# First slice of a two-layer block: chunk 5's masks and scaling moved ahead of lot 3's sign, and lower weights ahead of the next lot's sign

## The chip, the cores and the metric

The kernel runs on one core of a Trainium2 chip. The metric is the device time of one execution in microseconds (us). Before the change it is 591.01 us, the median of three runs (590.67 to 591.92).

Engines are named as the profile names them: PE is TensorE (matmuls; PEld its weight loads), DVE is VectorE, ACT is ScalarE, POOL is GpSimd, and SP issues most DMAs.

## What is computed

A linear attention with decay runs over 4 sequences of 8 heads and 768 positions. Its output, 3072 tokens by 512, goes through two matrix products with a squared ReLU between them.

```
for b in range(nb):                       # blocks of positions, per head
    intra = (qb @ kb.T * Dmask) @ vb      # Dmask[i, j] = lam ** (i - j) for i >= j
    inter = (qb * lam_pow) @ kv_state
    out[b] = intra + inter
    kv_state = lam_block * kv_state + (kb * rev_pow).T @ vb
x = out reshaped to (3072, 512)
g = relu(x @ w_in) ** 2                   # 3072 x 2048
return g @ w_out                          # 3072 x 512
```

## The kernel before

Positions are handled in chunks of 128, 6 to a sequence and 24 in all, and tokens in slices of 4 chunks (512 tokens). Each slice runs 16 iterations f over blocks of the 2048 hidden features: `hidden` (12 matmuls, line 521) makes h, `square` (ACT, lines 528 to 531) makes gh and the exact square, `rest` (DVE, line 536) their difference gl, and `project` (lines 551, 552, 556), one iteration later, adds to four output tiles. Every operand is held as a high and a low part (wh and wl, xh and xl, gh and gl), and three products are taken of them. A chunk's attention is spread over the iterations of the slice ahead: `scores` after step 0, `masked` (two masks on DVE, line 302, from PSUM) in step 1, `attend` in step 2.

The first slice (this loop, about 26 to 125 us) also splits the weights as they arrive, in 17 lots u, with u = f + 2 in iteration f. For a lot, SP loads `raw` (line 113); ACT takes the absolute value of its high words into A (`first_hi`, line 118) and scales the low words (`first_lo`, line 123); DVE works on A in four steps, `clamp` (L131), `shift` (L135), `sign` (L142) and `rounded` (L148), each of which needs the one before it; ACT then writes wh (`upper`, L154), and DVE wl = A - wh (`lower`, L157). `raw` and A have two buffers each, so lot u + 2 is loaded when rounded is done with lot u.

Each engine runs its instructions in the order in which this file issues them; nothing reorders them. The order is written out by hand. For f < 3 an iteration issues lower of the lot before, then clamp, shift, sign and rounded of its own lot, and upper after `rest`; from f = 3 on it issues clamp, shift and sign, then upper and lower of the lot before, then rounded.

POOL scales k and q of a chunk in place (`prep_k`, L296, and `prep_q`, L290) and the state (`decay`, L376). Where it may begin is held back by `turn` (L162), a copy of one element into `mark` on POOL: for f = 1 of A of the iteration's own lot, from f = 3 on of the lower weights just made. It stands ahead of the scaling in POOL's queue, so the scaling waits for what turn waits for. Chunk 4's scaling belongs to f = 1, chunk 5's q scaling to f = 5, chunk 6's k scaling to f = 8, and chunk 7's to f = 12 (k) and f = 13 (q).

Of the kernel before, what the change touches and what calls it, by code (L numbers as in the profile page):

```python
# [31 lines left out]
NLOT = NF + 1  # L32
# [3 lines left out]
def body(ctx: ExitStack, tc: tile.TileContext, qT, kT, kvq, lam, w, out):  # L36
# [31 lines left out]
    def load_qk(t):  # L68
        if t in (2, 3):
            lent[t] = wk.tile([P, 2, KT * C, 2], F32, name=f"lent{t}", tag=("xh", "xl")[t - 2])  # L70
            x = lent[t][:, 0].rearrange("p a b -> p (a b)")
        elif (t, 0) in lent:
            x = lent[t, 0]
        else:
            x = io.tile([P, 2 * DM], F32, name="qk_sb")
        feat[t] = x.rearrange("p (k a b) -> p k a b", k=2, a=NPR)
        for k, y in enumerate((kT, qT)):
            nc.sync.dma_start(out=feat[t][:, k], in_=y[t])

    def load_kv(t):  # L80
        if t in (2, 3):
            x = lent[t][:, 1].rearrange("p a b -> p (a b)")
        elif (t, 1) in lent:
            x = lent[t, 1]
        else:
            x = io.tile([P, 2 * DM], F32, name="kv_sb")
        nc.sync.dma_start(out=x, in_=kvq[t, :, 0 : 2 * DM])
        x = x.rearrange("p (k h d) -> p k h d", k=2, h=H)
        tok[t] = x[:, 0], x[:, 1]
# [8 lines left out]
    def lot(t, u):  # L98
        if u in (0, NF):
            return t[:, u : u + 1]  # L100
        return t.rearrange("p (s f) d -> p s f d", s=2)[:, :, u]
# [6 lines left out]
    def wload(u):  # L108
        if u < NLOT:
            x = pieces(u)  # L110
            raw[u] = wk.tile([P, len(x) * DM], I64, name="raw", tag="raw")
            for i, (side, f) in enumerate(x):
                nc.sync.dma_start(out=raw[u][:, i * DM : (i + 1) * DM], in_=w[side, :, f])

    def first_hi(u):
        r = raw.pop(u).bitcast(U32).rearrange("p (n two) -> p n two", two=2)
        A = wk.tile([P, r.shape[1]], U32, name="A")
        nc.scalar.activation(A.bitcast(F32), r[:, :, 1].bitcast(F32), AF.Abs)
        cv[u] = r[:, :, 0], r[:, :, 1], A

    def first_lo(u):
        L = cv[u][0]
        nc.scalar.activation(L, L, AF.Copy, scale=2.0**-29)
# [5 lines left out]
    def clamp(u):  # L129
        A = cv[u][2].bitcast(F32)  # L130
        V.tensor_scalar(out=A, in0=A, scalar1=2.0**-15, scalar2=float(LIM), op0=ALU.max, op1=ALU.min)  # L131

    def shift(u):
        A = cv[u][2]
        V.tensor_scalar(  # L135
            out=A, in0=A, scalar1=3, scalar2=0x3FFFFFFF,
            op0=ALU.logical_shift_left, op1=ALU.bitwise_and,
        )

    def sign(u):  # L140
        L, Hw, A = cv[u]
        V.scalar_tensor_tensor(  # L142
            out=A, in0=Hw, scalar=0xC0000000, in1=A, op0=ALU.bitwise_and, op1=ALU.bitwise_or
        )

    def rounded(u):
        L, Hw, A = cv[u]
        V.tensor_tensor(out=A, in0=A, in1=L, op=ALU.add)  # L148

    def whole(u):  # L150
        return cv[u][2].bitcast(F32).rearrange("p (a d) -> p a d", d=DM)

    def upper(u):
        nc.scalar.copy(lot(wh, u), whole(u))  # L154

    def lower(u):
        V.tensor_tensor(out=lot(wl, u), in0=whole(u), in1=lot(wh, u).bitcast(F32), op=ALU.subtract)  # L157
        cv.pop(u)

    def turn(u, half):  # L160
        x = cv[u][2].bitcast(F32)[0:1, 0:1] if half else wl[0:1, u, 0:1].bitcast(F32)
        nc.gpsimd.tensor_copy(mark[:, 0:1], x)  # L162
# [43 lines left out]
    for j in range(2):  # L206
# [5 lines left out]
        lambda o, x, y, op=op: V.tensor_tensor(out=o, in0=x, in1=y, op=op)  # L212
# [5 lines left out]
    b_, t_, u_, c_, d_, af = (sq[:, i, 0 : NS - 1] for i in range(6))  # L218
# [69 lines left out]
    def prep_q(t):  # L288
        if t % NCB:
            nc.gpsimd.tensor_tensor(out=feat[t][:, 1], in0=feat[t][:, 1], in1=qpow, op=ALU.mult)  # L290

    def prep_k(t):
        if t % NCB < NCB - 1:
            x = tok[t][0].rearrange("p (a j) d -> p a j d", j=2)
            y = mask.rearrange("p j a c -> p a j c")[:, :, :, C - 1 : C]
            nc.gpsimd.tensor_tensor(out=x, in0=x, in1=y.broadcast_to([P, NPR, 2, D]), op=ALU.mult)  # L296

    def masked(t):
        a_of[t] = []
        for j in range(2):  # L300
            a = wk.tile([P, NPR, C], F32, name="a", tag="gl" if t in (1, 3) else "a")
            V.tensor_tensor(
                out=a, in0=sc_of[t][j].rearrange("p (a b) -> p a b", a=NPR),
                in1=mask[:, j], op=ALU.mult,
            )
            a_of[t].append(a)
# [57 lines left out]
    def attend(t, pool, name):  # L364
        u = pool.tile([P, DM], F32, name=name)
        o = pool.tile([P, DM], F32, name=name)
        news(t, u)
        within(t, o, True, not t % NCB)
        before(t, o, False, True)
        update(t, u)  # L370
        return split(t, o)

    def decay(t):
        if t % NCB < NCB - 2:
            for j, r in enumerate(rows):
                nc.gpsimd.tensor_tensor(  # L376
                    out=kvd[r], in0=kv[r, :, rows[j]],
                    in1=qpow[r, :, C - 1 : C].broadcast_to([D, NPR, D]), op=ALU.mult,
                )
# [128 lines left out]
    def fade_state(second):  # L508
        d = kv[:, :, D:] if second else kv[:, :, 0:D]
        nc.gpsimd.tensor_tensor(  # L510
            out=kvd, in0=d, in1=qpow[:, :, D - 1 : D].broadcast_to([P, NPR, D]), op=ALU.mult
        )
# [3 lines left out]
    def hidden(m, f, xh, xl):  # L516
        h = ps_h.tile([P, N], F32, name="h")
        k = 0
        for wt, x in ((wh, xh), (wl, xh), (wh, xl)):
            for kt in range(KT):  # L520
                nc.tensor.matmul(  # L521
                    h, wt[:, f, kt * P : (kt + 1) * P], x[:, kt], start=k == 0, stop=k == 11
                )
                k += 1
        return h

    def square(h):
        nc.scalar.activation(h, h, AF.Relu)  # L528
        gh = wk.tile([P, N], F32R, name="gh")
        nc.scalar.activation(gh, h, AF.Square)  # L530
        nc.scalar.activation(h, h, AF.Square)  # L531
        return gh

    def rest(m, f, r, gh):
        gl = wk.tile([P, N], F32R, name="gl")
        V.tensor_tensor(out=gl, in0=r, in1=gh.bitcast(F32), op=ALU.subtract)  # L536
        g_of[m, f] = gh, gl
# [528 lines left out]
    for f in range(NF):  # L1066
        t, step, u_ = G + f // 4, f % 4, f + 2
        h = hidden(0, f, *xs_of[0])
        if f < 3:
            lower(u_ - 1)  # L1070
            for op in (clamp, shift, sign, rounded):
                op(u_)
            if f == 1:
                turn(u_, True)
        else:
            if u_ < NLOT:
                for op in (clamp, shift, sign):
                    op(u_)
            if f > 3:
                upper(u_ - 1)  # L1080
            lower(u_ - 1)
            if u_ - 1 < NF:
                turn(u_ - 1, False)
            if u_ < NLOT:
                rounded(u_)
        wload(u_ + 2)
        if f == 3:
            low[G]()
        if f == 0:
            decay(3)  # L1090
        if step == 0 and f or f == 1:
            prep_k(t)
        if step == 1:
            prep_q(t)
        if step == 3:
            if t < 2 * G - 1:
                decay(t)
            else:
                fade_state(False)
        gh = square(h)  # L1100
        rest(0, f, h, gh)
        if step == 1:
            masked(t)
        if f < 3:
            upper(u_)
            first_hi(u_ + 1)
        if step == 2:
            low[t] = attend(t, ps_a, "att")
            if t > G:
                low[t]()  # L1110
        if u_ + 1 < NLOT:
            if f >= 3:
                first_hi(u_ + 1)
            first_lo(u_ + 1)
        if prev is not None:
            project(*prev)
        prev = (0, f)
        if step == 2:
            load_qk(t + 2)
            load_kv(t + 2)  # L1120
        if step == 0:
            scores(t, ps_a, "att")
        if f == NF - 2:
            fold_mask()
            scale_k(t + 1)
        if f == NF - 1:
            open_half(t + 1)
            scale_k(t + 2)
# [30 lines left out]
    for f in range(NF):  # L1159
        t = first_t + f // 2  # L1160
# [54 lines left out]
    for f in range(NF):  # L1215
        t = first_t + f // 2
# [96 lines left out]
```

## Time and profile before

| | |
|---|---|
| median of 3 runs | 591.01 us |
| the profiled execution | 592.3 us |
| its span, first to last instruction | 590.5 us |
| granted TensorE clock over the span | 0.995 |
| DVE busy, 48.54 to 78.43 us | 29.52 of 29.89 us |
| DVE busy, 79.96 to 121.00 us | 40.52 of 41.04 us |

A row of a timeline gives the start in us from the span's start, the duration, the engine, the line of the kernel, the operation, output and inputs with their shapes, and how many instructions the row joins. A bracket at its end gives the time for which the engine sat idle ahead of it, and who released it. In a row of stretches each number is an engine's busy time, in the order PE, PEld, DVE, ACT, POOL; the clock, DMA's busy share and GB/s follow.

### The profile page before, as it was taken

What the parts mean: (1) busy time and instruction counts of PE and PEld (TensorE: products, weight loads), DVE (VectorE), ACT (ScalarE), POOL (GpSimd) and SP (SyncE); (2) the same over time, 40 slices, a digit from 0 to 9 for tenths busy, and PEclk for the clock granted to TensorE, in tenths of its full rate; (3) what the DMA queues carried; (4) which work ended last, traced back from release to release, by engine and by line L of the source; (5) the groups of instructions that cost most, each with busy time, mean ns of one, the idle gap of its engine ahead of it and who ended that gap; (6) DMA issues with size and microseconds to landing.
All of it is one profiled execution on the core that took longest, in us unless ns stands there. A gap on an engine that the chain in (4) does not pass through costs nothing.

```text
span 590.5 us, 12541 instructions
## 1 busy us (share of the span) xinstructions
PE 573.2 (97%) x5006; PEld 484.6 (82%) x5006; DVE 416.0 (70%) x684; ACT 272.3 (46%) x501; POOL 97.5 (17%) x106
## 2 busy tenths in 40 slices
PE   8989999999899999999999999999899999999996
PEld 6877887888788887878888887888688888999996
DVE  6899989956567675786666667577554456997943
ACT  4676876835254455433333334445533233642520
POOL 4420221433323231000000002355100000000000
PEclk9999999999899999999999999999999999999999
DMA  8766475326778695466666644632287665766863
GB/s 294 301 225 215 157 258 196 138 74 243 247 233 286 198 299 211 146 203 204 197 195 197 196 161 148 229 128 73 73 279 240 196 194 175 255 214 209 280 206 108
DMA packets 69386, 119.32 MB, mean 202 GB/s; under 512 B 6352, under 2 KB 30928, under 8 KB 69328
## 3 DMA queue, kind: packets, MB, share of 16 engines
q1 hardware_dynamic: 67152, 116.42, 60.1%
q10 hardware_dynamic: 2176, 2.10, 1.0%
q8 instruction: 40, 0.66, 0.4%
q14 instruction: 18, 0.15, 0.1%
HBM read 88.08 MB, written 29.36 MB: 199 GB/s over the span
## 4 chain that ended last, share of the span: by engine, by line
PE 75%; DVE 12%; issue 6%; ACT 3%; DMA 2%; POOL 1%; DVEq 0%; SPq 0%; POOLq 0%; ACTq 0%
PE h L681 17%; PE h L521 10%; PE acc L920 7%; PE acc L551 7%; PE acc L556 7%; PE acc L552 7%; PE att L681 7%; PE att L920 4%; PE att L442 3%; PE h L920 2%; DVE A L142 2%; DVE sums L212 1%; DVE A L148 1%; DVE wl L157 1%; DVE rec L212 1%
## 5 line engine op out<-in xcount | busy, mean ns | idle before, releaser
L551 PE MATMUL acc<-wh,gh 128*128 128x512 f32 x256 | 101.1, 395 | 0.0
L556 PE MATMUL acc<-wh,gl 128*128 128x512 f32 x256 | 99.9, 390 | 0.0
L552 PE MATMUL acc<-wl,gh 128*128 128x512 f32 x256 | 99.7, 390 | 0.0
L681 PE MATMUL h<-wh,ring 128*128 128x512 f32 x320 | 85.9, 390 | 0.6 <-DVE kv_sb L212 0.5
L528 ACT ACTIVATE h<-h 128x512 f32<-128x512 f32 x48 | 28.0, 583 | 99.6 <-PE h L521 40.2
L681 PEld LDWEIGHTS h<-wh,ring 128*128 128x128 f32 x320 | 59.8, 188 | 14.1 <-DVE kv_sb L212 1.3
L536 DVE TENSOR_TENSOR gl<-h,gh 128x512 fp32r<-128x512 f32 x48 | 32.9, 686 | 36.5 <-ACT h L531 36.5
L551 PEld LDWEIGHTS acc<-wh,gh 128*128 128x128 f32 x256 | 48.0, 188 | 10.9 <-issue 0.5
L556 PEld LDWEIGHTS acc<-wh,gl 128*128 128x128 f32 x256 | 48.1, 188 | 10.8 <-DVE gl L536 0.6
L552 PEld LDWEIGHTS acc<-wl,gh 128*128 128x128 f32 x256 | 48.1, 188 | 9.6
L681 PE MATMUL h<-wl,ring 128*128 128x512 f32 x160 | 49.3, 389 | 0.0
L510 POOL TENSOR_TENSOR kvd<-kv,qpow 128x256 f32<-128x256 f32 x27 | 23.2, 861 | 88.1 <-DVE kv L212 73.2
L521 PE MATMUL h<-xh,wh 128*128 128x512 f32 x128 | 36.5, 408 | 0.3 <-DVE a L212 0.2
L393 POOL TENSOR_TENSOR kv_sb<-kv_sb,mask 128x512 f32<-128x512 f32 x13 | 16.0, 1231 | 124.3 <-DMA kv_sb<-in_kvq 124.1
L521 PE MATMUL h<-xh,wl 128*128 128x512 f32 x128 | 34.6, 392 | 0.7 <-DVE wl L157 0.7
L920 PE MATMUL acc<-folds,wh 128*128 128x256 f32 x192 | 35.2, 283 | 0.0
L681 PEld LDWEIGHTS h<-wl,ring 128*128 128x128 f32 x160 | 30.0, 188 | 6.3
L521 PE MATMUL h<-xl,wh 128*128 128x512 f32 x128 | 34.2, 389 | 0.0
L681 PE MATMUL att<-wh,ring 128*128 128x512 f32 x128 | 34.2, 389 | 0.0
L212 DVE TENSOR_TENSOR wl<-sums,wh 128x1024 fp32r<-128x1024 f32 x24 | 29.2, 1218 | 2.4 <-ACT wh L892 1.9
L920 PEld LDWEIGHTS acc<-folds,wh 128*128 128x128 f32 x192 | 30.0, 192 | 0.0
L530 ACT ACTIVATE gh<-h 128x512 fp32r<-128x512 f32 x48 | 28.8, 600 | 1.5
(251 smaller groups left out, 1188.0 us busy)
## 6 DMA issues: line engine op xcount, KB each, us to landing
ring<-ws SPq DMA_DIRECT2D x112, 256.0 KB, 3.0
raw<-in_w SPq DMA_DIRECT2D x32, 512.0 KB, 4.4
folds<-wt SPq DMA_DIRECT2D x64, 256.0 KB, 3.6
kv_sb<-in_kvq SPq DMA_DIRECT2D x19, 512.0 KB, 6.0
ws<-parts SPq DMA_DIRECT2D x32, 256.0 KB, 3.8
qk_sb<-in_kT SPq DMA_DIRECT2D x20, 256.0 KB, 4.0
qk_sb<-in_qT SPq DMA_DIRECT2D x20, 256.0 KB, 4.4
out_x<-o SPq DMA_DIRECT2D x16, 256.0 KB, 5.1
```

The lines of the kernel that those rows point to most:

```text
L212: lambda o, x, y, op=op: V.tensor_tensor(out=o, in0=x, in1=y, op=op)
L442: nc.tensor.matmul(o[h][r, p * D : (p + 1) * D], x, y, start=(h, r.start) not in begun, stop=end, skip_group_check=True,)
L510: nc.gpsimd.tensor_tensor(out=kvd, in0=d, in1=qpow[:, :, D - 1 : D].broadcast_to([P, NPR, D]), op=ALU.mult)
L521: nc.tensor.matmul(h, wt[:, f, kt * P : (kt + 1) * P], x[:, kt], start=k == 0, stop=k == 11)
L528: nc.scalar.activation(h, h, AF.Relu)
L530: nc.scalar.activation(gh, h, AF.Square)
L536: V.tensor_tensor(out=gl, in0=r, in1=gh.bitcast(F32), op=ALU.subtract)
L551: nc.tensor.matmul(accs[m][i], gh[:, cs], wh[:, j], start=f == 0, stop=False)
L552: nc.tensor.matmul(accs[m][i], gh[:, cs], wl[:, j], start=False, stop=False)
L556: nc.tensor.matmul(accs[m][i], gl[:, cs], wh[:, j], start=False, stop=end)
L681: nc.tensor.matmul(bank, x[:, part_, kt], t[:, q + kt], start=start and z == 0, stop=stop and z == 5, skip_group_check=True,)
L920: nc.tensor.matmul(bank[:, r * 2 * P : (r + 1) * 2 * P], x, y, start=n == 0 and r == 0 and z == 0, stop=n == NQ - 1 and z == 2, skip_group ...
```

## The change

In f = 1 chunk 4's masks (called the fifth chunk in the change's own words, counted from one) and the turn that lets POOL scale its k and q stand right behind lot 3's shift, ahead of its sign and rounded; they were behind rounded and, for the masks, behind gl. From f = 3 on lower of the lot before stands ahead of the own lot's sign instead of behind it. No instruction is added or removed.

```diff
         if f < 3:
             lower(u_ - 1)
-            for op in (clamp, shift, sign, rounded):
-                op(u_)
+            clamp(u_)
+            shift(u_)
             if f == 1:
                 turn(u_, True)
+                masked(t)
+            sign(u_)
+            rounded(u_)
         else:
             if u_ < NLOT:
-                for op in (clamp, shift, sign):
-                    op(u_)
+                clamp(u_)
+                shift(u_)
             if f > 3:
                 upper(u_ - 1)
             lower(u_ - 1)
+            if u_ < NLOT:
+                sign(u_)
             if u_ - 1 < NF:
                 turn(u_ - 1, False)
             if u_ < NLOT:
                 rounded(u_)
...
         rest(0, f, h, gh)
-        if step == 1:
+        if step == 1 and f > 1:
             masked(t)
```

On DVE, in f = 1, lot 3's steps with the masks (`a`) of chunk 4; rows with - are those of before, with + those of the change:

```order
 L131 TENSOR_SCALAR A<-A 128x1024
 L135 TENSOR_SCALAR A<-A 128x1024
-L142 SCALAR_TENSOR_TENSOR A<-raw,A 128x1024
-L148 ISA A<-raw,A 128x2048
-L536 TENSOR_TENSOR gl<-h,gh 128x512
 L302 TENSOR_TENSOR a<-att,mask 128x512 x2
+L142 SCALAR_TENSOR_TENSOR A<-raw,A 128x1024
+L148 ISA A<-raw,A 128x2048
+L536 TENSOR_TENSOR gl<-h,gh 128x512
 L157 TENSOR_TENSOR wl<-A,wh 128x2x512
```

The two masks go past sign, rounded and gl; ahead of lower (L157), which needs ACT's upper of the same lot, there is now gl alone.

On DVE, in f = 5, before the change; A of the first two rows is lot 7's, and `wl` is made from lot 6:

```order
L131 TENSOR_SCALAR A<-A 128x1024
L135 TENSOR_SCALAR A<-A 128x1024
L142 SCALAR_TENSOR_TENSOR A<-raw,A 128x1024
L157 TENSOR_TENSOR wl<-A,wh 128x2x512
L148 ISA A<-raw,A 128x2048
L536 TENSOR_TENSOR gl<-h,gh 128x512
L302 TENSOR_TENSOR a<-att,mask 128x512 x2
```

The same place with the change:

```order
L131 TENSOR_SCALAR A<-A 128x1024
L135 TENSOR_SCALAR A<-A 128x1024
L157 TENSOR_TENSOR wl<-A,wh 128x2x512
L142 SCALAR_TENSOR_TENSOR A<-raw,A 128x1024
L148 ISA A<-raw,A 128x2048
L536 TENSOR_TENSOR gl<-h,gh 128x512
L302 TENSOR_TENSOR a<-att,mask 128x512 x2
```

Lower and sign have changed places, so rounded now stands right behind the sign that it needs. The turn is released by lower, as before. The order on PE, ACT, POOL and SP is the same as before; what changes there is when the instructions they wait for are done.

## The prediction

> **What bounds the kernel now.** I read the page's busy shares first, then busy time by stretches, then each engine's timeline from 29 to 121 us, where the changed loop runs.
>
> ```profile
> PE 573.2 (97%) x5006; PEld 484.6 (82%) x5006; DVE 416.0 (70%) x684; ACT 272.3 (46%) x501; POOL 97.5 (17%) x106
> ...
> 29.00:52.00 23.00, 21.33 (x140) 17.06 (x138) 21.04 (x24) 16.97 (x23) 3.48 (x5) 1.00 0.63 219
> 52.00:121.00 69.00, 68.33 (x413) 55.14 (x414) 66.64 (x80) 52.64 (x69) 17.99 (x18) 1.00 0.54 185
> ...
> 40.17 0.69 PE L317 MATMUL att<-kv_sb 128*64 128x64 f32 x16 [1.67 <-POOL kv_sb L296]
> 52.41 1.19 PE L521 MATMUL h<-xh,wl 128*128 128x512 f32 x4 [0.41 <-DVE wl L157]
> 54.86 0.19 PEld L556 LDWEIGHTS acc<-wh,gl 128*128 128x128 f32 x1 [0.32 <-DVE gl L536]
> 66.83 1.12 PE L325 MATMUL att<-a,kv_sb 128*64 128x128 f32 x15
> ```
>
> Over the whole span PE is the bound. In this loop that average misleads: a stretch lists busy PE, PEld, DVE, ACT and POOL, and DVE works 21.04 of 23.00 us and 66.64 of 69.00. PE waits 1.67 us for the scaled k (at 40.17), 0.41 for lower weights and 0.32 for gl, all of them released by DVE or by POOL after its turn, which DVE releases. The row at 66.83 has no wait, but the masks that it reads (65.64 in a fence below) end at 65.64 + 1.28 = 66.92, just as it starts. PE has no slack there: what DVE is late at chunk 5's masks, PE is late. Taking away PE's 1.67 us is a gain only if DVE also reaches the later points earlier.
>
> **Step 1, f = 1: masks, turn and scaling ahead of lot 3's sign.**
>
> ```profile
> 35.55 0.69 DVE L135 TENSOR_SCALAR A<-A 128x1024 uint32<-128x1024 uint32 x1
> 36.28 1.23 DVE L142 SCALAR_TENSOR_TENSOR A<-raw,A 128x1024 uint32<-128x1024 uint32 x1
> 37.64 1.23 DVE L148 CUSTOM_DVE_ANT_0 A<-raw,A 128x2048 uint16<-128x2048 uint16 x1
> 38.78 0.68 DVE L536 TENSOR_TENSOR gl<-h,gh 128x512 fp32r<-128x512 f32 x1
> 39.38 1.28 DVE L302 TENSOR_TENSOR a<-att,mask 128x512 f32<-128x512 f32 x2
> 40.58 1.87 DVE L157 TENSOR_TENSOR wl<-A,wh 128x1024 fp32r<-128x1024 f32 x1
> 42.37 0.68 DVE L131 TENSOR_SCALAR A<-A 128x1024 f32<-128x1024 f32 x1
> ...
> 38.93 0.17 POOL L162 COPY mark<-A 1x1 f32<-1x1 f32 x1 [8.80 <-DVE A L148]
> 39.07 1.05 POOL L296 TENSOR_TENSOR kv_sb<-kv_sb,mask 128x512 f32<-128x512 f32 x1
> 40.08 1.28 POOL L290 TENSOR_TENSOR qk_sb<-qk_sb,qpow 128x512 f32<-128x512 f32 x1
> ...
> 38.90 1.05 ACT L154 CAST wh<-A 128x1024 fp32r<-128x1024 f32 x1 [1.56 <-DVE A L148]
> ...
> 21.80 1.05 POOL L296 TENSOR_TENSOR lent<-lent,mask 128x512 f32<-128x512 f32 x1
> 21.82 2.13 DVE L142 SCALAR_TENSOR_TENSOR A<-raw,A 128x1024 uint32<-128x1024 uint32 x1
> ...
> 144.17 1.96 DVE L212 TENSOR_TENSOR parts<-sums,parts 128x1024 fp32r<-128x1024 f32 x1
> 145.00 1.60 POOL L510 TENSOR_TENSOR kvd<-kv,qpow 128x256 f32<-128x256 f32 x1
> 146.05 1.64 DVE L212 TENSOR_TENSOR rec<-wh,wl 128x1024 f32<-128x1024 f32 x1
> ```
>
> Nothing is removed; the question is what lies beside what. The last five rows show that DVE and POOL block each other. A sign that starts while POOL scales takes 2.13 us, not 1.23, and ends 23.95 - 22.85 = 1.10 after POOL. From 144 us they take turns: POOL's row at 145.00 ends (146.60) 0.47 after the DVE instruction that it waited behind (146.13), and the next one on DVE, started at 146.05, ends 1.09 after POOL. So what POOL has queued gets in at the end of a DVE instruction, ahead of the next. The masks read PSUM and are not stretched (1.28 beside the scaling at 39.07). Before, the k scaling and the first half of the q scaling lie beside gl and masks, and the rest of the q scaling stretches one lower to 1.87 (0.65 lost).
>
> After: the masks start 0.60 after the shift, as at 38.78 to 39.38, so at 36.15; the sign follows 1.20 later at 37.35. Its new wait for the turn costs nothing: the turn (0.17 us) runs beside the masks, and so does the k scaling. But the q scaling (1.28 us) is now due at about 37.45, and DVE has only sign and rounded to do, both on SBUF. Uncontended, rounded starts 1.36 after the sign, as 36.28 to 37.64. The loss by the q scaling lies between 0 (POOL always gives way) and 1.28 (all of it); I take 1.0, nearest to the 0.90 that the shorter scaling cost at 21.82. Rounded then ends at 37.35 + 1.36 + 1.0 + 1.23 = 40.94. ACT's upper (1.05) was hidden behind gl and masks; now only gl covers it. With 0.03 us for each handover, as 38.87 to 38.90, lower starts at 42.05; an unstretched lower occupies DVE for 1.14 (62.77 to 63.91 below), so the next clamp starts at 43.19 instead of 42.37: **+0.8** (bounds -0.2 to +1.1). PE gets its scaled k early, but then waits for gl and lower weights, which are later. Behind the later rounded, SP also issues the raw load of lot 5 later:
>
> ```profile
> 38.89 0.80 SPq L113 DMA_DIRECT2D raw<-in_w  x2
> raw<-in_w SPq DMA_DIRECT2D x32, 512.0 KB, 4.4
> 47.39 1.11 ACT L118 ACTIVATE A<-raw 128x1024 f32<-128x1024 f32 x1
> ```
>
> About 2.1 us later it lands near 38.89 + 2.1 + 4.4 = 45.4, still ahead of its reader at 47.39: nothing.
>
> **Step 2, f = 3 to 13: lower ahead of sign.** The pattern before, at f = 5, with POOL and ACT beside it:
>
> ```profile
> 60.90 0.69 DVE L135 TENSOR_SCALAR A<-A 128x1024 uint32<-128x1024 uint32 x1
> 62.77 1.22 DVE L157 TENSOR_TENSOR wl<-A,wh 128x1024 fp32r<-128x1024 f32 x1
> 63.91 1.22 DVE L148 CUSTOM_DVE_ANT_0 A<-raw,A 128x2048 uint16<-128x2048 uint16 x1
> 65.64 1.28 DVE L302 TENSOR_TENSOR a<-att,mask 128x512 f32<-128x512 f32 x2
> ...
> 64.12 1.04 POOL L162 COPY mark<-wl 1x1 f32<-1x1 f32 x1 [4.42 <-DVE wl L157]
> 65.12 1.30 POOL L290 TENSOR_TENSOR qk_sb<-qk_sb,qpow 128x512 f32<-128x512 f32 x1
> ...
> 60.78 1.03 ACT L154 CAST wh<-A 128x1024 fp32r<-128x1024 f32 x1
> ```
>
> Shift start to rounded start is 63.91 - 60.90 = 3.01 us. After: lower follows the shift, on which it does not depend, in 0.60, then sign in 1.14, then rounded, which needs that sign, in 1.36: 3.10. That is 0.09 a lot, 11 lots: **+1.0** (bounds 0 to 1.3). PE gets lower weights some 1.2 us earlier, which ends its 0.41 us wait; but gl and masks, which come after rounded, are later, so this counts nothing.
>
> Lower needs ACT's upper, and the sign no longer covers it. At f = 5 upper ends at 61.81 and lower would start at 60.90 + 0.60 = 61.50: 0.3 us lost, 0.25 after DVE's added 0.09. At f = 8:
>
> ```profile
> 79.96 0.69 DVE L131 TENSOR_SCALAR A<-A 128x1024 f32<-128x1024 f32 x1 [1.52 <-ACT A L118]
> 80.69 0.70 DVE L135 TENSOR_SCALAR A<-A 128x1024 uint32<-128x1024 uint32 x1
> 80.86 1.05 ACT L154 CAST wh<-A 128x1024 fp32r<-128x1024 f32 x1
> 84.91 1.05 POOL L296 TENSOR_TENSOR kv_sb<-kv_sb,mask 128x512 f32<-128x512 f32 x1
> 85.43 1.09 DVE L131 TENSOR_SCALAR A<-A 128x1024 f32<-128x1024 f32 x1
> ```
>
> Upper ends at 81.91, lower would start at 81.29: 0.65. Together **+0.9** (bounds 0 to 1.0). DVE's 1.52 us of idle time at 79.96 absorbs nothing: it waits for a raw load that is issued behind an earlier rounded, which is later as well.
>
> **Step 3: POOL's turn comes 1.2 us earlier in the lot.** At 64.12 the turn, released by lower, is held by rounded (1.04 us instead of 0.17), so the q scaling starts at 65.12, when DVE goes over to gl and masks from PSUM. After, the instruction behind lower is the sign. The turn is held until the sign ends; then DVE pauses 0.13 us (1.36 - 1.23) before rounded, and POOL's scaling gets in first, as POOL did at 146.1 with no pause at all. Rounded waits for it: 1.28 less what the pause and the start hide, about 1.0 at f = 5 and at f = 13: **+2.0** (bounds 0 to 2.6). The k scaling at f = 8 and f = 12 (1.05) costs about 0.8 in the same way, where before it stretched a clamp by 0.40 (1.09 for 0.69): **+0.8** (bounds -0.8 to 1.3).
>
> No row has rounded itself starting under POOL; the nearest is the sign. A rule speaks to it: the Trainium skill, "SBUF — State Buffer", "Who interferes with whom", says that a DVE instruction with two SBUF inputs contends with a GpSimd instruction that reads SBUF, and that whichever issues first holds the pair for its whole length. By it, rounded (two SBUF inputs) is blocked in full and the sum below stands or rises by the 0.3 that I took off each q scaling; if rounded were exempt, the sum would be near 1.5. The trace agrees where it can: 2.13 us for a sign, 1.28 for masks.
>
> The last masks that bind are those of chunk 7:
>
> ```profile
> 116.52 1.28 DVE L302 TENSOR_TENSOR a<-att,mask 128x512 f32<-128x512 f32 x2
> 118.04 1.04 PE L325 MATMUL att<-a,kv_sb 128*64 128x128 f32 x16
> ```
>
> They end at 117.80, so PE has 0.24 of slack: -0.2. **Sum**: 0.8 + 1.0 + 0.9 + 2.0 + 0.8 - 0.2 = +5.3 us, which PE carries on, as it is 97% busy. The profiled execution took 592.3 us (span 590.5), 1.3 above the median of 591.0; against it the sum is 597.6, against the median **596.3 us**.
>
> **Rivals.** (a) *Rounded gets in ahead of POOL.* If the pause of 0.13 us is too short for POOL, scaling stays beside gl and masks as before; step 1 gives -0.2 and step 3 nothing: -0.2 + 1.0 + 0.9 - 0.2 = +1.5, so 592.5. For it: the pause is short. Against: at 146.1 POOL got in where DVE made no pause. (b) *Nothing measurable.* As (a), with the uppers early enough too: +0.6, so 591.6. (c) *Faster.* PE's waits of 1.67 and 0.41 are gone and do not come back: 591.0 - 2.1 = 588.9. The place that decides is the gl before 54.86: it would have to be ready 2.1 us earlier, by 52.8, and the masks of chunk 5 by 64.8. For it: DVE shows 66.64 of 69.00 us, not all. Against: DVE's work is not less, and its cover for one upper is gone. (d) *The change does not do what it says:* the k scaling still comes late. Its load and scores are done long before, so I give this nothing of its own.
>
> **Chances.** Main case 0.60; (a) 0.20, of which 0.12 slower and 0.08 within the bound; (b) 0.08; (c) 0.12. Slower by over 0.2% (1.2 us, about what a measurement of this kernel can tell from no change) 0.72, within 0.16, faster 0.12. The range leaves out (c) and the main case's upper tail with all bounds at their ends: 590.6 to 597.8.
>
> **What would show it.** PE's wait of 1.67 us before L317 gone; L290 of chunk 4 beside sign or rounded, one of these near 2.2 us; the turns ending with the sign; rounded near 2.2 us at f = 5 and f = 13; PE waiting for a before L325 of chunks 5 to 7. If rounded stays at 1.23 everywhere, (a) holds. If DVE shows idle time between 52 and 78, DVE was not the bound and I am wrong.

## The result and the profile after

The change makes the kernel slower: 595.04 us, median of 6 runs (594.27 to 598.66), against 590.84 (588.86 to 591.92) for six runs of before. The ratio is 1.0061, 95% interval 1.0035 to 1.0086, or +3.6 us (2.1 to 5.1). The profiled execution took 594.67 us with a span of 592.9. The forecast was 596.3 us: right in direction, somewhat too large.

The line of busy times from the page after, and from its groups the matmuls that read gl (`project`, L556); PE waits 2.2 us ahead of them, where this group had no such wait before:

```profile
PE 573.7 (97%) x5006; PEld 483.7 (82%) x5006; DVE 419.8 (71%) x684; ACT 272.7 (46%) x501; POOL 100.1 (17%) x106
...
L556 PE MATMUL acc<-wh,gl 128*128 128x512 f32 x256 | 100.3, 392 | 2.2 <-DVE gl L536 2.2
```

PE's busy time is what it was (573.2). DVE has 3.8 us more and POOL 2.6 us more with the same number of instructions: instructions were stretched, none added.

In f = 1 (DVE, then POOL, of the kernel after):

```profile
36.17 1.28 DVE L302 TENSOR_TENSOR a<-att,mask 128x512 f32<-128x512 f32 x2
37.37 1.23 DVE L142 SCALAR_TENSOR_TENSOR A<-raw,A 128x1024 uint32<-128x1024 uint32 x1
38.73 2.08 DVE L148 CUSTOM_DVE_ANT_0 A<-raw,A 128x2048 uint16<-128x2048 uint16 x1
40.73 0.68 DVE L536 TENSOR_TENSOR gl<-h,gh 128x512 fp32r<-128x512 f32 x1
41.92 1.23 DVE L157 TENSOR_TENSOR wl<-A,wh 128x1024 fp32r<-128x1024 f32 x1 [0.51 <-ACT wh L154]
43.07 0.69 DVE L131 TENSOR_SCALAR A<-A 128x1024 f32<-128x1024 f32 x1
```

```profile
36.46 1.05 POOL L296 TENSOR_TENSOR kv_sb<-kv_sb,mask 128x512 f32<-128x512 f32 x1
37.48 2.25 POOL L290 TENSOR_TENSOR qk_sb<-qk_sb,qpow 128x512 f32<-128x512 f32 x1
```

The k scaling lies beside the masks at no cost. The q scaling is queued beside the sign, is held until the sign ends (37.37 + 1.23 = 38.60), and ends at 39.73. Rounded, which would follow the sign at 38.73, is held in turn: 2.08 us instead of 1.23, ending 1.08 after POOL. Masks, sign and lower stand where the prediction put them, within 0.13 us; the next clamp starts at 43.07, where 43.19 was forecast and 42.37 was before.

In f = 5 (again DVE and POOL of after):

```profile
62.72 1.23 DVE L157 TENSOR_TENSOR wl<-A,wh 128x1024 fp32r<-128x1024 f32 x1 [0.33 <-ACT wh L154]
63.87 1.22 DVE L142 SCALAR_TENSOR_TENSOR A<-raw,A 128x1024 uint32<-128x1024 uint32 x1
65.12 2.34 DVE L148 CUSTOM_DVE_ANT_0 A<-raw,A 128x2048 uint16<-128x2048 uint16 x1
67.98 1.27 DVE L302 TENSOR_TENSOR a<-att,mask 128x512 f32<-128x512 f32 x2
```

```profile
64.08 1.04 POOL L162 COPY mark<-wl 1x1 f32<-1x1 f32 x1 [4.83 <-DVE wl L157]
65.09 1.29 POOL L290 TENSOR_TENSOR qk_sb<-qk_sb,qpow 128x512 f32<-128x512 f32 x1
```

The turn ends with the sign (65.12 beside 65.09), the q scaling goes first, and rounded, started at 65.12, ends 1.08 after POOL does (67.46 beside 66.38). The same picture stands at the other three places where POOL scales behind a turn, here the rows of rounded in f = 8, 12 and 13:

```profile
84.89 2.10 DVE L148 CUSTOM_DVE_ANT_0 A<-raw,A 128x2048 uint16<-128x2048 uint16 x1
...
111.04 2.10 DVE L148 CUSTOM_DVE_ANT_0 A<-raw,A 128x2048 uint16<-128x2048 uint16 x1
...
117.53 2.33 DVE L148 CUSTOM_DVE_ANT_0 A<-raw,A 128x2048 uint16<-128x2048 uint16 x1
```

And on PE of after, the wait for the scaled k is gone, and others have come:

```profile
38.47 0.69 PE L317 MATMUL att<-kv_sb 128*64 128x64 f32 x16
...
47.76 0.50 PE L556 MATMUL acc<-wh,gl 128*128 128x512 f32 x1 [0.55 <-DVE gl L536]
...
51.85 1.19 PE L521 MATMUL h<-xh,wl 128*128 128x512 f32 x4 [0.62 <-DVE wl L157]
...
55.67 0.50 PE L556 MATMUL acc<-wh,gl 128*128 128x512 f32 x1 [1.25 <-DVE gl L536]
...
68.71 0.43 PE L325 MATMUL att<-a,kv_sb 128*64 128x128 f32 x2 [1.00 <-DVE a L302]
...
121.17 0.69 PE L317 MATMUL att<-kv_sb 128*64 128x64 f32 x16 [1.66 <-issue]
121.72 1.09 PE L325 MATMUL att<-a,kv_sb 128*64 128x128 f32 x16
```

The 1.67 us that PE saved at L317 it pays back by 55.67: it waits 0.55 us for gl, 0.62 for lower weights (0.41 before) and 1.25 for gl. Counted from the clamp of f = 0 in each kernel, this last matmul starts 0.8 us later than before (55.67 - 27.94 beside 54.86 - 27.93). From there PE loses what DVE is late at two of the three masks: 1.00 us at chunk 5's (68.71), nothing at chunk 6's, and 1.66 at chunk 7's. The profile names no releaser for this last wait. That it is for the masks is read from the times: L317 starts 0.78 us behind the start of the masks' row (120.39), and so it does in e2, e3 and e4 below, the other kernels with a wait there.

### The profile page after: what moved, and what is told of

It reads as the page before. It is cut to its first block, busy times and chain, and to the rows that moved or that the text cites. A ratio compares the mean times of both kernels' runs of the same rounds, so it can differ in the third digit from the quotient of the medians.

```text
span 592.9 us, 12539 instructions
## 1 busy us (share of the span) xinstructions
PE 573.7 (97%) x5006; PEld 483.7 (82%) x5006; DVE 419.8 (71%) x684; ACT 272.7 (46%) x501; POOL 100.1 (17%) x106
## 4 chain that ended last, share of the span: by engine, by line
PE 74%; DVE 10%; DMA 5%; issue 5%; ACT 3%; SPq 1%; POOL 1%; DVEq 0%; POOLq 0%; ACTq 0%
PE h L681 18%; PE h L521 9%; PE acc L551 8%; PE acc L920 7%; PE acc L556 7%; PE acc L552 7%; PE att L681 7%; PE att L920 4%; PE att L442 2%; DMA raw<-in_w 2%; DMA qk_sb<-in_kT 2%; PE h L920 2%; DVE sums L212 1%; DVE A L142 1%; DVE A L148 1%
## 5 line engine op out<-in xcount | busy, mean ns | idle before, releaser
L556 PE MATMUL acc<-wh,gl 128*128 128x512 f32 x256 | 100.3, 392 | 2.2 <-DVE gl L536 2.2
L556 PEld LDWEIGHTS acc<-wh,gl 128*128 128x128 f32 x256 | 48.0, 188 | 14.0 <-DVE gl L536 4.0
```

What stands on the lines that cost most here:

```text
L556: nc.tensor.matmul(accs[m][i], gl[:, cs], wh[:, j], start=False, stop=end)
```

## Experiments

Eight kernels were run in two groups. Each of the seven variants was timed twelve times beside before; e0 is a second profile of before.

| run | median us | before beside it | ratio (95%) | in us |
|---|---|---|---|---|
| after (the change) | 595.04 | 590.84 | 1.0061 (1.0035 to 1.0086) | +3.6 |
| e1 masks only | 593.29 | 592.17 | 1.0010 (0.9992 to 1.0029) | +0.6 |
| e2 lower only | 594.02 | 592.17 | 1.0043 (1.0022 to 1.0064) | +2.5 |
| e3 turn held | 592.91 | 592.17 | 1.0017 (0.9997 to 1.0036) | +1.0 |
| e6 one collision | 593.79 | 592.17 | 1.0027 (1.0005 to 1.0049) | +1.6 |
| e4 held, q late | 592.70 | 591.60 | 1.0028 (1.0012 to 1.0044) | +1.7 |
| e5 masks, q late | 592.25 | 591.60 | 1.0023 (1.0003 to 1.0044) | +1.4 |
| e7 all masks | 592.63 | 591.60 | 1.0030 (1.0012 to 1.0048) | +1.8 |

The ratio is not the quotient of the two medians; by these the differences are 1.1, 1.9, 0.7, 1.6, 1.1, 0.7 and 1.0 us for the seven variants in the order of the table, all within the intervals. The intervals are some 2 to 3 us wide, so they tell "all of it" from "none of it" but hardly one step from the next. For steps the traces are compared: start of the same instruction in two kernels, each counted from its own clamp of f = 0, a DVE instruction ahead of all that the edits move.

### Before, profiled again

The change's trace is only 2.4 us behind the trace of before that the prediction was worked from (span 592.9 and 590.5), while the medians stand 4.2 us apart. So before was profiled once more.

> The kernel before once more, for its profile: whether the raw load of lot 10, issued behind rounded at 71.8 us, again takes about 7 us to reach its reader at f = 7, and whether the clock is again below 1.00 somewhere between 121 and 160 us. If the load takes 5 us here, the 1.5 us that the changed kernel made up ahead of f = 8 are chance of one profile; if 7, they belong to when that load meets the loads of chunk 7.

It took 590.29 us, span 588.6: 1.9 us less than its first profile. One load accounts for DVE's part. First the profile from which the prediction was made, rounded of lot 8 (which frees the raw buffer) and the first reader of lot 10's raw words:

```profile
70.56 1.22 DVE L148 CUSTOM_DVE_ANT_0 A<-raw,A 128x2048 uint16<-128x2048 uint16 x1
...
78.81 1.12 ACT L118 ACTIVATE A<-raw 128x1024 f32<-128x1024 f32 x1 [2.46 <-DMA raw<-in_w]
```

The same two in the second profile of before, with its clamp of f = 0 and, at the end, chunk 7's masks and the matmuls that read them:

```profile
28.35 0.69 DVE L131 TENSOR_SCALAR A<-A 128x1024 f32<-128x1024 f32 x1
...
71.00 1.22 DVE L148 CUSTOM_DVE_ANT_0 A<-raw,A 128x2048 uint16<-128x2048 uint16 x1
...
77.26 1.17 ACT L118 ACTIVATE A<-raw 128x1024 f32<-128x1024 f32 x1 [0.46 <-DMA raw<-in_w]
...
115.43 1.28 DVE L302 TENSOR_TENSOR a<-att,mask 128x512 f32<-128x512 f32 x2
...
117.94 1.05 PE L325 MATMUL att<-a,kv_sb 128*64 128x128 f32 x16
```

From the end of rounded to ACT's start: 78.81 - 71.78 = 7.0 us in the first profile, 77.26 - 72.22 = 5.0 in the second (5.2 in after; 5.1 to 5.4 in e2 to e6; 6.3 in e7 and 7.5 in e1). DVE's 1.52 us of idle time at 79.96 was this one slow load, and in the second profile it is not there. So PE's slack at chunk 7's masks is 117.94 - (115.43 + 1.28) = 1.23 us here, not 0.24. Loads as slow come in other traces too (e1, e7), so a typical execution may lie between these two. What follows is measured against this second profile. In after the same masks are

```profile
27.94 0.69 DVE L131 TENSOR_SCALAR A<-A 128x1024 f32<-128x1024 f32 x1
...
120.39 1.27 DVE L302 TENSOR_TENSOR a<-att,mask 128x512 f32<-128x512 f32 x2
```

DVE is late by (120.39 - 27.94) - (115.43 - 28.35) = 5.37 us, and PE (121.72 and 117.94 in the same way) by 4.19: the 5.37 less the slack of 1.23, which is now 0.06. Spans differ by 592.9 - 588.6 = 4.3.

### Each part alone

e1 has f = 1's part only (its edit against before, as for e2 and e6):

```diff
-            for op in (clamp, shift, sign, rounded):
-                op(u_)
+            clamp(u_)
+            shift(u_)
             if f == 1:
                 turn(u_, True)
+                masked(t)
+            sign(u_)
+            rounded(u_)
...
-        if step == 1:
+        if step == 1 and f > 1:
             masked(t)
```

> Only the f = 1 part (masks and turn ahead of lot 3's sign); lower stays behind sign from f = 3 on. Port theory (POOL's scaling gets in ahead of rounded): rounded of lot 3 takes about 2.1 us as in the changed kernel, the clamp of lot 4 starts 0.7 us later than before, nothing collides from f = 3 on, so the masks of chunk 5 start about 0.7 us later than at 65.64 and the time is 0.5 to 0.8 us above before. Rival (the order of DVE alone costs, the port nothing): 0.2 us below to 0.2 above before. Second rival (PE's removed wait of 1.67 us is a gain that the other part of the change loses again): 1 to 1.7 us below before.

e2 has the other part only:

```diff
-                for op in (clamp, shift, sign):
-                    op(u_)
+                clamp(u_)
+                shift(u_)
             if f > 3:
                 upper(u_ - 1)
             lower(u_ - 1)
+            if u_ < NLOT:
+                sign(u_)
```

> Only lower ahead of sign from f = 3 on; f = 1 as before. Port theory: rounded takes about 2.3 us at f = 5 and f = 13 and 2.1 at f = 8 and f = 12; masks of chunk 5 start 1.5 us later than before, PE waits for them, and the time is 2.5 to 3.5 us above before. Rival (order alone): rounded stays near 1.23 everywhere, the time is 0.5 to 1.3 us above before from the pause between sign and rounded and from the uncovered upper.

Rounded of f = 1 in e1, and of f = 5 in e2:

```profile
38.63 2.09 DVE L148 CUSTOM_DVE_ANT_0 A<-raw,A 128x2048 uint16<-128x2048 uint16 x1
```

```profile
65.04 2.33 DVE L148 CUSTOM_DVE_ANT_0 A<-raw,A 128x2048 uint16<-128x2048 uint16 x1
```

Each part brings its own collision by itself. The times, +0.6 us (-0.5 to +1.7) and +2.5 (1.3 to 3.8), add up to 3.1, within the interval of the whole. Most of the loss is in the order of lower and sign. e1's interval holds zero: that f = 1 makes DVE late by itself is seen in its trace (chunk 5's masks 0.7 us later than in e0), that it costs time is not shown. Nor does PE of this trace give a price. At chunk 5 PE is 2.2 us later than in e0, and it lost this in one place:

```profile
53.03 1.64 PE L521 MATMUL h<-xh,wl 128*128 128x512 f32 x4 [1.89 <-DVE wl L157]
```

PE, which has its k early, waits 1.89 us for lower weights that come 0.7 us later than in e0. The other 1.5 us are lost right behind: from 53 to 57 us the granted clock is 0.57 (1.00 in e0).

### Is it the collision? The turn held back

e3 is the whole change, with the turn behind rounded from f = 3 on, reading A of the own lot, so that POOL begins when rounded ends (its edit against the change).

```diff
             if u_ < NLOT:
                 sign(u_)
-            if u_ - 1 < NF:
-                turn(u_ - 1, False)
             if u_ < NLOT:
                 rounded(u_)
+                turn(u_, True)
```

> The whole change, but from f = 3 on the turn waits for rounded of the iteration's own lot instead of for lower, so that POOL scales beside gl and masks again. Port theory: rounded takes 1.23 us at f = 5, 8, 12 and 13 (2.1 remains at f = 1), masks of chunk 5 start about 1.3 us later than before (2.34 in the changed kernel), and the time is 1 to 1.8 us above before, some 2 to 2.5 below the changed kernel. Rival (order alone): within 0.5 us of the changed kernel, 3.5 to 4.5 above before.

In f = 5 of e3, DVE and POOL:

```profile
64.60 1.23 DVE L148 CUSTOM_DVE_ANT_0 A<-raw,A 128x2048 uint16<-128x2048 uint16 x1
...
66.35 1.28 DVE L302 TENSOR_TENSOR a<-att,mask 128x512 f32<-128x512 f32 x2
```

```profile
65.96 0.17 POOL L162 COPY mark<-A 1x1 f32<-1x1 f32 x1 [5.57 <-DVE A L148]
66.10 1.30 POOL L290 TENSOR_TENSOR qk_sb<-qk_sb,qpow 128x512 f32<-128x512 f32 x1
```

Rounded is back at 1.23 us, the turn at 0.17, and the scaling lies beside the masks. By the times this gives back 2.6 of the 3.6 us, known to about 2 us only (+1.0 is left, interval -0.2 to +2.1). The traces are sharper: on PE at chunk 7 the change is 4.19 us later than e0, e3 1.35, which is 2.84 less. So the collision from f = 3 on is the largest part of the loss, near the 2.8 us that the prediction gave to q and k scalings.

e6 puts one such collision into before: only in f = 5, the turn waits for lot 7's sign and stands ahead of lower.

```diff
             if u_ < NLOT:
                 for op in (clamp, shift, sign):
                     op(u_)
+            if f == 5:
+                turn(u_, True)
...
-            if u_ - 1 < NF:
+            if u_ - 1 < NF and f != 5:
                 turn(u_ - 1, False)
```

> The kernel before, with one edit: at f = 5 the turn waits for the sign of lot 7 instead of for lower of lot 6, so it is held by lower and POOL's q scaling is due right ahead of rounded. Port theory: rounded of lot 7 takes about 2.3 us instead of 1.22, the masks of chunk 5 start about 1.0 us later, PE waits for them about 1.0 us, and the time is 0.8 to 1.2 us above before; by the masks of chunk 6 DVE has caught up 0 to 1 us, as it has an idle stretch of 1.52 us ahead of f = 8, but PE does not get back what it waited. Rival (order alone, DVE's lateness is absorbed): rounded at 1.23, time as before within 0.3 us.

POOL, then DVE and PE of e6:

```profile
62.89 1.04 POOL L162 COPY mark<-A 1x1 f32<-1x1 f32 x1 [3.28 <-DVE A L142]
63.90 1.28 POOL L290 TENSOR_TENSOR qk_sb<-qk_sb,qpow 128x512 f32<-128x512 f32 x1
```

```profile
63.97 2.29 DVE L148 CUSTOM_DVE_ANT_0 A<-raw,A 128x2048 uint16<-128x2048 uint16 x1
...
67.52 0.43 PE L325 MATMUL att<-a,kv_sb 128*64 128x128 f32 x2 [0.67 <-DVE a L302]
```

One collision stretches rounded to 2.29 us and brings chunk 5's masks 1.24 us later than in e0. PE waits 0.67 us for them and is 1.2 us late at chunk 7, where DVE is 1.7 us late and no longer the one that is waited for (its masks end 0.8 us ahead of their reader): what PE has lost at chunk 5 it doesn't get back. The time, +1.6 us (0.3 to 2.9), agrees. The collision alone is a cause, without any other part of the change.

### Without the collision in f = 1

e5 is e1 with the k scaling behind the masks and the q scaling held by a second turn behind rounded, e4 the same on top of e3 (the edit against e1 and against e3).

```diff
             if f == 1:
                 turn(u_, True)
                 masked(t)
+                prep_k(t)
             sign(u_)
             rounded(u_)
+            if f == 1:
+                turn(u_, True)
+                prep_q(t)
...
-        if step == 0 and f or f == 1:
+        if step == 0 and f:
             prep_k(t)
-        if step == 1:
+        if step == 1 and f > 1:
             prep_q(t)
```

> Only the f = 1 part, with the q scaling behind a second turn that waits for rounded; from f = 3 on as before. Port theory: clamp of lot 4 0.1 to 0.2 us earlier than before, PE's wait of 1.67 us gone, and the time within 0.3 us of before, since DVE's masks of chunk 5 still set PE's pace. Rival (PE's wait is worth its 1.67 us): 1 to 1.7 us below before.

> The whole change with the turn held by rounded from f = 3 on (as in the run before), and in f = 1 the k scaling right behind the shift but the q scaling behind a second turn that waits for rounded. Port theory: no rounded is stretched in f = 1 either (1.23 instead of 2.1), the clamp of lot 4 starts 0.2 us earlier than before instead of 0.7 later, the masks of chunk 5 0.2 to 0.4 us later than before; the time is 0 to 0.8 us above before. What is left is the price of the order alone (pause between sign and rounded, uncovered uppers). Rival (order alone is the whole loss): 3 us or more above before.

In f = 1 of e4, DVE's lower and PE's first matmul on the scaled q:

```profile
41.13 1.52 DVE L157 TENSOR_TENSOR wl<-A,wh 128x1024 fp32r<-128x1024 f32 x1 [0.51 <-ACT wh L154]
...
41.62 1.09 PE L332 MATMUL att<-qk_sb,kv 128*64 128x128 f32 x16 [1.54 <-POOL qk_sb L290]
```

Rounded is short again (1.22 us), but the late q scaling now stretches lower to 1.52, and PE waits 1.54 us for q where it waited 1.67 for k. The wait has only moved. e4 misses its expectation: the next clamp starts 0.13 us later than before's, counted from f = 0, instead of 0.2 earlier (in e5 0.12 later), and the time is +1.7 us (0.7 to 2.6), above what was expected. No scaling of k or q stretches rounded in e4, and its PE is still 1.12 us late at chunk 7: what is left there is the order of lower and sign, with the uppers that lower waits for, and the wait for q. In e5 PE is 0.12 us late at the same place, so nearly nothing; its time, +1.4 us (0.2 to 2.6; 0.65 by the medians), is above the 0.3 that was expected. That is not explained by its first slice and stays open (the last section has a candidate).

### An attempt at a faster kernel

e7 puts the masks behind the shift in every f that has them, changes lower and sign in f = 3 and f = 11 alone, with the turn held there, and takes the gl of f = 3 ahead of the other low part (the main part of its edit against before).

```diff
+            swap = f in (3, 11)
             if u_ < NLOT:
-                for op in (clamp, shift, sign):
-                    op(u_)
+                clamp(u_)
+                shift(u_)
+                if step == 1:
+                    masked(t)
+                if not swap:
+                    sign(u_)
...
             lower(u_ - 1)
-            if u_ - 1 < NF:
+            if swap:
+                sign(u_)
+            elif u_ - 1 < NF:
                 turn(u_ - 1, False)
             if u_ < NLOT:
                 rounded(u_)
+            if swap:
+                turn(u_, True)
```

f = 1 is as in e5.

> A version meant to beat both: f = 1 as in the run with the late q scaling; the masks of chunks 5, 6 and 7 also right behind the shift, so that PE never waits for them; lower ahead of sign only at f = 3 and f = 11, where PE waited for lower weights, with the turn behind rounded there; the low part of chunk 4's x behind gl at f = 3. Port theory with DVE as the bound only where PE reads gl, lower weights or masks: no rounded above 1.3, no wait of PE for masks, gl of f = 3 ready about 0.7 us earlier, lower weights at f = 11 no longer waited for; PE reaches the end of the first slice 0.7 to 1.2 us earlier than before and the time is 0.5 to 1.3 us below before. Rival (DVE's total work bounds the loop): within 0.3 us of before.

It is a miss: +1.8 us (0.7 to 2.8). The waits between 29 and 150 us in e7 (total, times, longest):

```profile
ACT A L118 <- DMA raw<-in_w: 12.9, 8, 2.9
...
DVE A L131 <- ACT A L118: 3.7, 3, 2.1
...
PE h L521 <- DVE wl L157: 2.6, 3, 1.7
```

DVE waits 3.7 us for ACT (1.2 in e0's trace), and PE 2.6 us for lower weights (0.4). Why is open. With masks ahead of rounded, rounded ends later (1.3 us at f = 5), and with it the raw buffer comes free later. But the longest of DVE's waits, 2.1 us, stands behind one slow load: lot 11's raw words reach ACT 7.9 us after rounded of lot 9, against 5.3 in e0, and rounded itself is 0.7 us late there. ACT's total of 12.9 us does not decide it either: it is 7.0 in e0, but 12.5 in the change's own trace, where DVE waits 0.8 us for ACT. None of the variants beats before.

## Why the prediction was right, and where it was off

**What bounds.** Right: DVE bounds this loop, and PE follows it. DVE's delay of 5.37 us at chunk 7's masks less the slack gives PE's 4.2.

**Step 1.** Right: +0.70 measured (clamp at 43.07 instead of 42.37), +0.8 forecast, by the mechanism named. ACT's upper is uncovered as said (0.51 us of idle time ahead of lower).

**Step 2, the order.** This term was wrong: 0.09 us a lot was worked out from a pause of 1.36 us between a sign's start and rounded's. In the new order that pause does not come back. These are lot 6's sign and rounded in f = 4 of after:

```profile
57.99 1.22 DVE L142 SCALAR_TENSOR_TENSOR A<-raw,A 128x1024 uint32<-128x1024 uint32 x1
59.24 1.22 DVE L148 CUSTOM_DVE_ANT_0 A<-raw,A 128x2048 uint16<-128x2048 uint16 x1
```

59.24 - 57.99 = 1.25. Shift to rounded takes 3.00 us from f = 4 on, where it was 3.01: only f = 3 has the 0.08. The term is about 0.1 in place of 1.0.

**Step 2, the uppers.** Right in kind, too small: 0.41 us at f = 5 and 0.47 at f = 8 (0.25 and 0.65 forecast), and 0.32 at f = 9 and 0.15 at f = 13, which the prediction had not seen, together 1.35 for 0.9. The waits of DVE in the loop of after, and of e0 (two fences, the same view):

```profile
DVE wl L157 <- ACT wh L154: 2.0, 5, 0.5
```

```profile
DVE wl L157 <- ACT wh L154: 0.5, 1, 0.5
```

One of the five, for lot 2's lower, is there in both. The others are new: lot 3's (41.92), which belongs to step 1, and those in f = 5, 8 and 9; in f = 13 the delay is too short to be listed.

**Step 3.** Right: the q scalings cost 1.12 and 1.11 us (2.34 and 2.33 instead of 1.22), 2.23 for 2.0; the k scalings 2 times 0.88 less the 0.41 by which a clamp is no longer stretched, 0.94 for 0.8. (In e0 the first of these clamps is not stretched but starts 0.49 us late behind ACT, which makes it 0.86.) The state's decay (L376) in f = 11 adds 0.14 in the same way (0.45 on rounded, at 1.67, less 0.31 that it cost a shift before), and had no term. The rule of the Trainium skill, "SBUF — State Buffer", "Who interferes with whom", that was weighed there holds in kind: rounded, with two SBUF inputs, is blocked for 1.1 of the scaling's 1.28 us, between the 1.0 that the sum took and the whole length that the rule gives.

**The slack.** This term was wrong too: 0.2 us was taken off, and e0 has 1.23. Behind it is the sentence that DVE's 1.52 us of idle time at 79.96 absorbs nothing. Idle time that one slow load put into that profile was read as part of the kernel.

**The sum.** On DVE 0.70 + 0.1 + 1.35 + 2.23 + 0.86 + 0.14 = 5.4, beside 5.37 read at the masks; less 1.23 of slack it gives about 4.2, the difference of the medians of the change and of before (3.6 by the ratio). The forecast had 5.5 on DVE too, but this is partly luck: its order was 0.9 too large, its uppers, scalings and decay together 0.9 too small. Its surplus is the slack.

**Rivals.** (a) is out: POOL gets in ahead of rounded at each of the five places, with DVE's pause of 0.13 us in f = 1 and of 0.03 to 0.04 in the other four. (c) fell where the prediction said that it would be decided: the gl before L556 came later (PE waits 1.25 us for it at 55.67), not 2.1 us earlier. (b) and (d) are out by the time and by L317 at 38.47, which has no wait left.

**The signs.** PE waits for the masks of chunk 5 and, by the times, of chunk 7, but not of chunk 6. Between 52 and 78 us DVE idles once, 0.33 us at 62.72, for the upper that step 2 had counted.

## What to carry to other kernels

Where two engines share memory and one holds the other out, ask of every moved instruction what the other engine has queued at that moment, not only what it waits for: here most of the loss came from a marker of one element, released one instruction earlier, that let a scaling in ahead of an instruction from SBUF instead of one from PSUM. A wait that is taken away on the bounding engine is a gain only if the engine that feeds it is earlier at the next meeting points as well. Slack and idle time of a few tenths up to two microseconds, on which a sum rests, want a second profile of the same kernel.

## What the runs showed of the hardware

- At the five places here a queued POOL instruction got in between two DVE instructions, even where DVE pauses for 0.03 us only (sign 63.87 + 1.22 = 65.09, rounded at 65.12 and stretched to 2.34 us). The 1 x 1 copy of the turn is held by DVE in the same way: 1.04 us beside a sign, 0.17 when nothing holds it.
- The raw load of lot 10 took 7.0 and 5.0 us between the buffer's release and its reader in two profiles of the same kernel. Why one is slow is open.
- Behind PE's wait for gl at L409, near 150 us, the granted clock drops in some executions. In the first profile of before, the wait and the stretch behind it (its length, busy PE, PEld, DVE, ACT and POOL, with counts, then clock, DMA's share and GB/s):

```profile
150.67 0.69 PE L409 MATMUL h<-qk_sb 64*64 64x64 f32 x30 [1.92 <-DVE gl L536]
...
150.00:156.00 6.00, 5.33 (x119) 4.76 (x120) 2.93 (x6) 2.66 (x8) 1.04 (x2) 0.72 0.58 200
```

  and in the second:

```profile
150.03 0.69 PE L409 MATMUL h<-qk_sb 64*64 64x64 f32 x30 [1.38 <-DVE gl L536]
...
150.00:156.00 6.00, 5.82 (x127) 5.03 (x128) 2.31 (x4) 2.89 (x10) 1.87 (x2) 1.00 0.76 248
```

  The clock is 0.72 behind a wait of 1.92 us and 1.00 behind 1.38. In six traces with waits of 1.2 to 1.5 us there (after, e0, e2, e3, e4, e7) it stayed at 1.00; with 1.9 (before, e1) and 2.7 us (e5) it fell to 0.57 to 0.66 between 152 and 156 us; in e6 a wait of 1.9 us went without a drop. e1's wait of 1.89 us at 53.03, with 0.57 behind it, is a fourth drop. Before's first profile is 0.5 us behind its second at chunk 7 and 1.9 at the end, so up to 1.4 us of it may come from here. It is one part of why profiles of one kernel differ, and may be part of e5's unexplained time; no run isolates it.
